# Input products of the state-space part for two chunks at once, and a closing sum moved

## The chip, the cores and the metric

The kernel runs on one core of one Trainium2 chip. The metric is the device time of one execution in microseconds (us), the median of several runs. Engines are named as in the profile: PE (TensorE, the matrix products), DVE (VectorE), ACT (ScalarE), POOL (GpSimd) and SP (SyncE, which issues most DMAs). L300 is line 300 of the kernel before.

## The reference

Two operators act on the same input x (2048 tokens by 1024 features), and a gate for each token mixes them.

```python
g = sigmoid((x * gate_w).sum(-1, keepdims=True))
a = irfft2(rfft2(x) * (w_r + 1j * w_i))            # a spectral filter over tokens and features
Lam_bar = exp(dt * Lam);  B_bar = ((Lam_bar - 1) / Lam)[:, None] * Bmat
Bu = einsum("bld,pd->blp", x, B_bar)               # 1024 complex states
h[t] = Lam_bar * h[t-1] + Bu[t]                    # 2048 steps
b = 2 * einsum("blp,dp->bld", h, Cmat).real + x * Dskip
return g * a + (1 - g) * b
```

The output is 2048 x 1024 in bfloat16.

## The kernel before, in words

**The spectral part** (`gfnet`) is a chain of short transforms. A front over 16 rows j turns x into the layout xQ (`turn_x`, PE transposes with a copy on ACT), folds it (DVE), and makes two transforms (`fd`, `s1`). `fd` leaves X1 by a copy out of PSUM (L339), on DVE for rows 3, 5 and 7 and on ACT for the others. `s1` leaves A (L351), on DVE for the first eight rows and on ACT for the last eight, and SP stores A to DRAM (L353). Four buffers hold A of the last eight rows, so A of row 12 waits until A of row 8 is stored. Then come 16 groups g of the inverse transform over tokens (`is1`), each with loads of the filter W, two products with it on DVE ("quotients", L468 and L469) and a store; then 16 half groups (`is2`), which leave ZT. From ZT, `spectral` makes the result for one tile of 128 tokens: eight products (L601), a scaled copy on ACT (L604) and four adds on DVE (L606 to L610).

**The state-space part** cuts the 2048 tokens into 8 chunks c of 256 and the 1024 states into two halves q, so that there are 16 quarters (c, q). `unit(c, q)` makes B x for one quarter in two steps (real and imaginary part): 4 blocks of 8 products of 256 columns (L300) into a PSUM buffer of 128 x 1024, and one copy on ACT into the tile h (L302). Two such PSUM buffers alternate (`psu`), and `early` and `spectral` take theirs from the same two. After the second step seven pieces of DVE work go onto the list `work`: `turn_back` (rotate by the angle of each state, L262, L263), `join`, two scans (L275), `carry_on` (the state carried into the next chunk), `turn` (rotate forth and scale, L286, L287), `join_on` (L292, L293). Then h is ready. Six tiles of h go round.

**Output.** For a tile tb of 128 tokens, which belongs to chunk tb // 2, `c_half` multiplies h by C: 16 products of 512 columns (L570) and 4 for the skip term (L574), for each half of the 1024 features. Tiles 0 to 9 are done by `early`: the result is scaled on ACT (L588) and stored to a scratch in DRAM. Their spectral sum is closed later by `late_tile`: `spectral` for that tile, and a DMA on POOL's queue that adds the scratch (L616); `close` stores it. These are the ten closing sums. Tiles 10 to 15 are done by `own_tile` at the end, with their spectral result added in PSUM, or on DVE for the last two.

**Order.** On PE, DVE and ACT the instructions run in the order in which the program writes them; the order on POOL and SP is a scheduler's. The generator `ssm` strings units and early tiles together, and the loops over the spectral part take one step of it (`halves(ssm, 1)`) at fixed places. `vector(us)` issues pieces from `work` until their noted costs make up that many microseconds; `vector_until(c)` issues what chunk c still needs. After `ssm` is used up, `spectral` for tile 10 is written ahead of the last units, and then:

```python
for _ in chain(unit(7, 0)):
    vector(4.0)
for n in (1, 1):
    halves(last, 1)          # last = unit(7, 1)
    vector(4.0)
    close_early(n)           # n closing sums
```

After that each half of an output tile is followed by `vector(4.0)` and by one closing sum or none.

`make_tab` makes tables of angles and decays for the quarters, and with them rz (L215, L216), the decay of each state along a chunk, on POOL.

Of the kernel before, what the change touches and what calls it, by code (L numbers as in the profile page):

```python
# [13 lines left out]
FP32 = mybir.dt.float32  # L14
BF16 = mybir.dt.bfloat16
# [8 lines left out]
P = 128  # L24
TC = 256
# [3 lines left out]
NHA, NHB = 4, 2  # L29
# [79 lines left out]
def kernel(  # L109
# [17 lines left out]
    nc = tc.nc  # L127
# [40 lines left out]
    pools = {"u": psF}  # L168
# [15 lines left out]
    BT = [btp.tile([P, 2, 8, P], BF16, name=f"BT{jb}") for jb in range(8)]  # L184
# [23 lines left out]
    def make_tab(jp):  # L208
        sh = [P, 2, TC]
        js = slice(2 * jp, 2 * jp + 2)  # L210
        ang = tmp.tile(sh, FP32, name="ang")
        for j in range(2):
            nc.vector.tensor_scalar_mul(out=ang[:, j], in0=tau_f, scalar1=thp[:, 2 * jp + j:2 * jp + j + 1])
            jb = 2 * jp + j
            nc.gpsimd.tensor_copy(out=rz[:, jb, :], in_=r_sb[:, jb:jb + 1].to_broadcast([P, TC]))  # L215
            nc.gpsimd.memset(rz[:, jb, 0:1], 0.0)  # L216
        sn_f = tmp.tile(sh, FP32, name="sn_f")
        cs_f = tmp.tile(sh, FP32, name="cs_f")
        yield from sincos(tmp, ang, sh, sn_f, cs_f, "rot")
        nc.gpsimd.tensor_copy(out=tab[:, 1, js, :], in_=sn_f)  # L220
        t1 = tmp.tile(sh, FP32, name="t1")
        t2 = tmp.tile(sh, FP32, name="t2")
        for j in range(2):
            nc.scalar.activation(out=t1[:, j], in_=sn_f[:, j], func=ACT.Copy, scale=ci[:, 2 * jp + j:2 * jp + j + 1])
        yield
        nc.gpsimd.tensor_copy(out=tab[:, 0, js, :], in_=cs_f)
        for j in range(2):
            jb = 2 * jp + j
            nc.scalar.activation(out=t2[:, j], in_=cs_f[:, j], func=ACT.Copy, scale=ci[:, jb:jb + 1])
            nc.vector.scalar_tensor_tensor(out=tab[:, 2, jb, :], in0=cs_f[:, j], scalar=cr[:, jb:jb + 1], in1=t1[:, j],  # L230
                                           op0=ALU.mult, op1=ALU.subtract)
        yield
        for j in range(2):
            jb = 2 * jp + j
            nc.vector.scalar_tensor_tensor(out=tab[:, 3, jb, :], in0=sn_f[:, j], scalar=cr[:, jb:jb + 1], in1=t2[:, j],
                                           op0=ALU.mult, op1=ALU.add)

    rz = tabp.tile([P, 8, TC], FP32, name="rz")
# [1 line left out]
    ck = cpool.tile([P, 2, 2, 8], FP32, name="ck")  # L240
    hs = {}
    hpool = [hpA, None]
    hcount = [0]

    def halloc(shape, dtype):
        pool = hpool[hcount[0] % (NHA + NHB) >= NHA]
        hcount[0] += 1
        return pool.tile(shape, dtype, name="h")

    work = []  # L250
    x_t = xQ.rearrange("p d j (g q) -> p d g j q", g=2)

    def unit(c, q):
        sh = [P, 2, 4, TC]
        u = halloc(sh, BF16)
        js = slice(4 * q, 4 * q + 4)
        bc = lambda i: tab[:, i:i + 1, js, :].to_broadcast(sh)
        tmps = {}

        def turn_back():  # L260
            su = up.tile(sh, BF16, name="su")
            nc.vector.tensor_mul(out=su, in0=u[:, ::-1], in1=bc(1))  # L262
            nc.vector.tensor_mul(out=u, in0=u, in1=bc(0))  # L263
            tmps["su"] = su

        def join():
            su = tmps["su"]
            nc.vector.tensor_add(out=u[:, 0], in0=u[:, 0], in1=su[:, 0])
            nc.vector.tensor_sub(out=u[:, 1], in0=su[:, 1], in1=u[:, 1])
            if c:  # L270
                nc.vector.tensor_add(out=u[:, :, :, 0], in0=u[:, :, :, 0], in1=carry[:, :, js])

        def scan(ri):
            seg = u[:, ri].rearrange("p j t -> p (j t)")
            nc.vector.tensor_tensor_scan(out=seg, data0=rz[:, js].rearrange("p j t -> p (j t)"), data1=seg,  # L275
                                         initial=0.0, op0=ALU.mult, op1=ALU.add)

        def carry_on():
            if c + 1 < NCH:
                gl = u[:, :, :, TC - 1]  # L280
                nc.vector.tensor_mul(out=ck[:, :, :, js], in0=gl.unsqueeze(1).to_broadcast([P, 2, 2, 4]), in1=rot[:, :, :, js])
                nc.vector.tensor_add(out=carry[:, :, js], in0=ck[:, :, 0, js], in1=ck[:, :, 1, js])

        def turn():
            sg = up.tile(sh, BF16, name="sg", tag="su")
            nc.vector.tensor_mul(out=sg, in0=u[:, ::-1], in1=bc(3))  # L286
            nc.vector.tensor_mul(out=u, in0=u, in1=bc(2))  # L287
            tmps["sg"] = sg

        def join_on():  # L290
            sg = tmps["sg"]
            nc.vector.tensor_add(out=u[:, 0], in0=u[:, 0], in1=sg[:, 0])  # L292
            nc.vector.tensor_sub(out=u[:, 1], in0=u[:, 1], in1=sg[:, 1])  # L293
            hs[c, q] = u

        for ri in range(2):
            psu = pools["u"].tile([P, 4, TC], FP32, name="psu", tag="psu")
            for j in range(4):
                for d8 in range(8):
                    nc.tensor.matmul(psu[:, j, :], lhsT=BT[4 * q + j][:, ri, d8, :],  # L300
                                     rhs=x_t[:, d8, :, :, 8 * c:8 * (c + 1)], start=(d8 == 0), stop=(d8 == 7))
            nc.scalar.copy(out=u[:, ri].rearrange("p b (q j) -> p b q j", j=32),  # L302
                           in_=psu.rearrange("p b (j q) -> p b q j", j=32))
            if ri == 1:
                work.extend([(2.4, turn_back), (1.5, join), (2.3, lambda: scan(0)), (2.3, lambda: scan(1)),
                             (0.4, carry_on), (2.4, turn), (1.4, join_on)])
            yield 3.5

    owed = [0.0]

    def vector(us):
        owed[0] += us
        while work and owed[0] > 0:
            cost, piece = work.pop(0)
            piece()
            owed[0] -= cost
        if not work:
            owed[0] = min(owed[0], 0.0)
# [8 lines left out]
    def gfnet():  # L327
# [4 lines left out]
        def fd(j):  # L332
            ps = psA.tile([P, 2, K], FP32, name="ps_fd", tag="ps")
            for cls in range(2):
                for d4 in range(4):
                    nc.tensor.matmul(ps[:, cls, :], lhsT=preTs[j][:, 4 * cls + d4, :], rhs=G_sb[:, cls, d4, :],  # L336
                                     start=(d4 == 0), stop=(d4 == 3))
            X1 = gta.tile([P, 2, K], BF16, name="X1")
            (nc.vector.tensor_copy if j in (3,5,7,) else nc.scalar.copy)(out=X1.rearrange("p r (i c) -> p r i c", c=2), in_=ps.rearrange("p c (r i) -> p r i c", r=2))  # L339
            X1s[j] = X1  # L340

        def s1(j):
# [236 lines left out]
    def early(tb):  # L579
        psy = pools["u"].tile([P, D], FP32, name="ps_y", tag="psu")  # L580
        for hf in range(2):
            c_half(psy, tb, hf)
            if hf == 0:
                load_xs(tb + 1)
                yield 3.7
        for hf in range(2):
            ye = fft["lp"].tile([P, K], FP32, name="ye", bufs=2)
            nc.scalar.activation(out=ye, in_=psy[:, K * hf:K * (hf + 1)], func=ACT.Copy, scale=omg[:, tb:tb + 1])  # L588
            nc.sync.dma_start(out=y_dram[tb, hf], in_=ye)
        yield 3.7  # L590
# [157 lines left out]
    def chain(*items):  # L748
        for item in items:
            yield from item  # L750
# [2 lines left out]
        for _ in range(n):  # L753
            next(gen, None)

    ssm = chain(unit(0, 0), unit(0, 1), unit(1, 0), unit(1, 1), unit(2, 0), early(0), unit(2, 1), early(1), unit(3, 0), early(2), unit(3, 1), early(3), unit(4, 0), early(4), unit(4, 1), early(5), unit(5, 0), early(6), unit(5, 1), early(7), unit(6, 0), unit(6, 1), early(8), early(9))

    order = {
        **{j: [(load_B, n)] for j, n in ((2, 1), (3, 1), (4, 1), (5, 2), (6, 2), (7, 2), (8, 2), (9, 2))},
# [45 lines left out]
    nc.vector.scalar_tensor_tensor(out=thp, in0=dt, scalar=INV2PI, in1=lim, op0=ALU.mult, op1=ALU.mult)  # L805
    r_sb = sp.tile([P, 8], FP32, name="r_sb")
    nc.scalar.activation(out=r_sb, in_=are, func=ACT.Exp)
    tau_f = tmp.tile([P, TC], FP32, name="tau_f")
    nc.vector.tensor_copy(out=tau_f, in_=tau_i)

# [103 lines left out]
            yield v  # L914

    ga[NEARLY] = spectral(NEARLY, grat, own_home(NEARLY))
    last = unit(7, 1)

    def close_early(n):
        for _ in range(n):  # L920
            close(2)
            late_tile(late.pop(0))

    for _ in chain(unit(7, 0)):
        vector(4.0)
    for n in (1, 1):
        halves(last, 1)
        vector(4.0)
        close_early(n)
    for tb in range(NEARLY + 1, 16):  # L930
        xs[tb] = xQ.rearrange("p d (k j) m -> p (d k) (j m)", k=2)[:, tb].rearrange("p (d m) -> p d m", m=P)
        nc.sync.dma_start_transpose(out=xs[tb], in_=x[P * tb:P * (tb + 1), :])
    for tb, counts in ((10, (1, 1)), (11, (1, 1)), (12, (1, 1)), (13, (1, 1)), (14, (0, 0)), (15, (0, 0))):
        for _, n in zip(own(tb), counts):
            vector(4.0)
            close_early(n)
            if not late:
                close(0)
# [31 lines left out]
```

## Time and profile before

| | |
|---|---|
| median of 5 runs | 341.35 us (340.33 to 342.35) |
| profiled execution | 342.25 us, of which the span of the profile is 340.5 us |
| granted clock of PE | 0.998 |
| busy: PE, DVE, ACT, POOL | 327.7, 291.5, 166.9, 32.6 us |
| PE products of 256 columns (L300) | 1024 |
| copies of 128 x 1024 out of PSUM behind them (L302) | 32, 1011 ns each |

Stages, in us of the span: the front to about 88.7, a stretch of small steps to 126.4, the 16 groups of `is1` to about 203, `is2` and the rest of `ssm` to 262, the last units to 279.5, the output tiles 10 to 15 to 336.9, the last store to 340.5.

How the lines are read: a group line gives engine, operation, output and inputs with their shapes, count, busy time, mean length of one, and the idle time of the engine just before. A timeline line gives start, length, engine, line and operation, count, and in brackets how long the engine had stood idle before it and what released it. Lengths of products overlap, since they are pipelined; the spacing of starts is what one costs. The chain of work that ended last gives start and length of each piece.

### The profile page before, as it was taken

The page shows a single profiled execution, that of the slowest core. Times are in us where ns is not written, and L with a number is a line of the kernel's source. Part 1 is how long each engine was busy: PE and PEld are TensorE (multiplying, and loading weights), DVE is VectorE, ACT ScalarE, POOL GpSimd, SP SyncE. Part 2 cuts the span into 40 slices and gives each one's busy share as a digit, 9 for nine tenths or more (in the row PEclk, how much of TensorE's full clock was granted, in tenths as well). Part 3 has the DMA queues.
Part 4 walks back from the last instruction along what each step waited for, and adds up shares of the span by engine and source line. Part 5 has one row for each costly group of instructions (what it writes and reads, how often), then busy time and mean ns, then how long its engine had stood idle before and what let it go on. Part 6 is the DMA issues. An engine that isn't in the chain of part 4 may idle for free.

```text
span 340.5 us, 6233 instructions
## 1 busy us (share of the span) xinstructions
PE 327.7 (96%) x2446; PEld 212.0 (62%) x2446; DVE 291.5 (86%) x449; ACT 166.9 (49%) x211; POOL 32.6 (10%) x64
## 2 busy tenths in 40 slices
PE   7989899969999999999999999999999999999995
PEld 3445465746858584756666485869955875565552
DVE  2679949969999999999999999999980997999951
ACT  3697597834432145765566452546632242433410
POOL 1372012120000000000000000000000011122220
PEclk9999999999999999999999999999999999999999
DMA  7999999999996036988999954948103109946695
GB/s 264 379 206 150 231 224 208 124 188 240 257 274 118 2 92 177 227 227 228 268 233 295 233 155 128 239 130 218 62 2 102 54 22 142 178 93 109 107 141 169
DMA packets 83581, 58.71 MB, mean 172 GB/s; under 512 B 54328, under 2 KB 74304, under 8 KB 83424
## 3 DMA queue, kind: packets, MB, share of 16 engines
q1 hardware_dynamic: 80304, 55.64, 66.8%
q0 software_dynamic: 3168, 2.66, 8.2%
q8 instruction: 19, 0.31, 0.4%
q14 instruction: 10, 0.08, 0.1%
q10 hardware_dynamic: 80, 0.01, 0.0%
HBM read 30.49 MB, written 17.83 MB: 142 GB/s over the span
## 4 chain that ended last, share of the span: by engine, by line
PE 70%; DVE 21%; DMA 3%; ACT 2%; issue 2%; SPq 1%; DVEq 0%; ACTq 0%
PE ps_y L570 26%; PE psu L300 22%; PE ps_h L570 4%; DVE h L275 4%; PE ps_id L601 4%; PE ps_is L509 2%; PE ps_is L485 2%; PE ps_s L460 2%; PE ps_is L484 2%; DVE CT L351 2%; PE ps_fd L336 2%; DMA G_sb<-c_G 2%; PE ps_y L574 2%; DMA turn_scratch<-A 1%; DVE h L263 1%
## 5 line engine op out<-in xcount | busy, mean ns | idle before, releaser
L300 PE MATMUL psu<-xQ,BT 128*128 128x256 bf16 x1024 | 116.6, 273 | 0.8 <-ACT ye L588 0.5
L300 PEld LDWEIGHTS <-BT 128*128 128x128 bf16 x1024 | 98.9, 98 | 17.5 <-issue 4.5
L570 PE MATMUL ps_y<-CT,h 128*128 128x512 bf16 x448 | 101.3, 379 | 0.0
L570 PEld LDWEIGHTS <-h 128*128 128x128 bf16 x512 | 49.6, 98 | 55.2
L275 DVE TENSOR_TENSOR_SCAN h<-rz,h 128x1024 bf16<-128x1024 f32 x32 | 72.2, 2280 | 0.3
L302 ACT CAST h<-psu 128x1024 bf16<-128x1024 f32 x32 | 32.3, 1011 | 51.4 <-PE psu L300 51.3
L616 POOL DMA_DIRECT2D BT<-y_scratch x10 | 11.9, 1194 | 239.6 <-DVE BT L610 232.0
L588 ACT ACTIVATE ye<-ps_y,omg 128x512 f32<-128x512 f32 x20 | 12.7, 684 | 43.1 <-PE ps_y L574 28.7
L336 PE MATMUL ps_fd<-G_sb,preT 128*128 128x512 bf16 x128 | 30.4, 379 | 1.9 <-ACT X L339 1.0
L262 DVE TENSOR_TENSOR su<-h,tab 128x2048 bf16<-128x2048 bf16 x16 | 19.6, 1223 | 2.8 <-ACT h L302 2.2
L336 PEld LDWEIGHTS <-preT 128*128 128x128 bf16 x128 | 12.0, 98 | 15.6 <-issue 3.1
L462 ACT CAST X<-ps_s 128x1024 bf16<-128x1024 f32 x16 | 16.2, 1014 | 8.6 <-PE ps_s L460 8.6
L263 DVE TENSOR_TENSOR h<-h,tab 128x2048 bf16<-128x2048 bf16 x16 | 19.6, 1225 | 0.8
L287 DVE TENSOR_TENSOR h<-h,tab 128x2048 bf16<-128x2048 bf16 x16 | 19.6, 1225 | 0.5
L286 DVE TENSOR_TENSOR sg<-h,tab 128x2048 bf16<-128x2048 bf16 x16 | 19.5, 1218 | 0.1
L657 ACT COPY xQ<-pt 128x1024 bf16<-128x1024 bf16 x16 | 15.6, 1016 | 2.3 <-PE pt L656 2.2
L511 ACT CAST ZT<-ps_is 128x1024 bf16<-128x1024 f32 x16 | 15.5, 1023 | 2.2 <-PE ps_is L509 2.2
L339 ACT CAST X<-ps_fd 128x1024 bf16<-128x1024 f32 x13 | 13.2, 1014 | 6.1 <-PE ps_fd L336 6.1
L487 ACT CAST C<-ps_is 128x1024 bf16<-128x1024 f32 x16 | 16.1, 1008 | 0.0
L601 PE MATMUL ps_id<-raw,ZT 128*128 128x256 bf16 x128 | 15.9, 273 | 0.0
L570 PE MATMUL ps_h<-CT,h 128*128 128x512 bf16 x64 | 14.5, 379 | 0.0
L601 PEld LDWEIGHTS <-ZT 128*128 128x128 bf16 x128 | 12.4, 98 | 2.2
(186 smaller groups left out, 363.6 us busy)
## 6 DMA issues: line engine op xcount, KB each, us to landing
y_scratch<-ye SPq DMA_DIRECT2D x20, 256.0 KB, 2.7
CT<-in_A_x_dram SPq DMA_DIRECT2D x8, 512.0 KB, 6.1
Bb<-turn_scratch SPq DMA_DIRECT2D x16, 256.0 KB, 4.0
turn_scratch<-C SPq DMA_DIRECT2D x16, 256.0 KB, 3.8
raw<-turn_scratch SPq DMA_DIRECT2D x16, 256.0 KB, 4.0
Wb<-in_A_w_r_dram SPq DMA_DIRECT2D x32, 127.8 KB, 4.0
Wb<-in_A_w_i_dram SPq DMA_DIRECT2D x32, 127.8 KB, 4.0
out_dram<-BT SPq DMA_DIRECT2D x14, 256.0 KB, 3.1
```

Of the source, the lines that this page charges most:

```text
L262: nc.vector.tensor_mul(out=su, in0=u[:, ::-1], in1=bc(1))
L263: nc.vector.tensor_mul(out=u, in0=u, in1=bc(0))
L275: nc.vector.tensor_tensor_scan(out=seg, data0=rz[:, js].rearrange("p j t -> p (j t)"), data1=seg, initial=0.0, op0=ALU.mult, op1=ALU.add)
L286: nc.vector.tensor_mul(out=sg, in0=u[:, ::-1], in1=bc(3))
L287: nc.vector.tensor_mul(out=u, in0=u, in1=bc(2))
L300: nc.tensor.matmul(psu[:, j, :], lhsT=BT[4 * q + j][:, ri, d8, :], rhs=x_t[:, d8, :, :, 8 * c:8 * (c + 1)], start=(d8 == 0), stop=(d8 == 7))
L302: nc.scalar.copy(out=u[:, ri].rearrange("p b (q j) -> p b q j", j=32), in_=psu.rearrange("p b (j q) -> p b q j", j=32))
L336: nc.tensor.matmul(ps[:, cls, :], lhsT=preTs[j][:, 4 * cls + d4, :], rhs=G_sb[:, cls, d4, :], start=(d4 == 0), stop=(d4 == 3))
L462: nc.scalar.copy(out=X2, in_=ps2)
L487: nc.scalar.copy(out=C1.rearrange("p h (c i) -> p h c i", c=2), in_=psc.rearrange("p h (i c) -> p h c i", c=2))
L570: nc.tensor.matmul(psy, lhsT=hs[c, jb // 4][:, ri, jb % 4, P * tq:P * (tq + 1)], rhs=CT[ri][:, jb, 512 * dh:512 * (dh + 1)], start=(i == 0 ...
L601: nc.tensor.matmul(pse[:, slot, :], lhsT=ZT_t[:, i, tb, :], rhs=fft["Gi"][:, i, :], start=(kb == 0), stop=(kb == 1))
```

## The change

From chunk 2 on, `pair(k, q)` takes the place of the units of chunks 2k and 2k + 1. It has four steps (real and imaginary part, each with two of the four blocks), each of 16 products of 512 columns, which are the tokens of both chunks in one, and two copies on ACT, one into h of each chunk. The DVE work of both chunks goes onto `work` after the fourth step, that of chunk 2k first. The order of the quarters on DVE becomes (2,0), (3,0), (2,1), (3,1), (4,0), (5,0), (4,1), (5,1), (6,0), (7,0), (6,1), (7,1). The number of steps in `ssm` is 48 as before. Early tiles now come two after another. Which of the six tiles of h a quarter takes is written in a table. The last pair is (3, 1), with a closing sum behind its second, third and fourth step; tile 13 has one less. X1 is copied by ACT in all rows. rz is written in one place ahead of the tables.

```diff
-            jb = 2 * jp + j
-            nc.gpsimd.tensor_copy(out=rz[:, jb, :], in_=r_sb[:, jb:jb + 1].to_broadcast([P, TC]))
-            nc.gpsimd.memset(rz[:, jb, 0:1], 0.0)
...
-    def halloc(shape, dtype):
-        pool = hpool[hcount[0] % (NHA + NHB) >= NHA]
-        hcount[0] += 1
-        return pool.tile(shape, dtype, name="h")
+    slots = {(0, 0): 0, (0, 1): 1, (1, 0): 2, (1, 1): 3, (2, 0): 4, (3, 0): 5, (2, 1): 0, (3, 1): 1,
+             (4, 0): 2, (5, 0): 3, (4, 1): 4, (5, 1): 0, (6, 0): 5, (7, 0): 1, (6, 1): 2, (7, 1): 4}
+
+    def halloc(c, q, shape, dtype):
+        slot = slots[c, q]
+        return hpool[slot >= NHA].tile(shape, dtype, name="h", tag=f"h{slot}", bufs=1)
...
+    def pair(k, q):
+        both = [pieces(2 * k + i, q) for i in range(2)]
+        for ri in range(2):
+            for h in range(2):
+                psu = pools["u"].tile([P, 2, 2 * TC], FP32, name="psu", tag="psu")
+                for j in range(2):
+                    for d8 in range(8):
+                        nc.tensor.matmul(psu[:, j, :], lhsT=BT[4 * q + 2 * h + j][:, ri, d8, :],
+                                         rhs=x_t[:, d8, :, :, 16 * k:16 * (k + 1)], start=(d8 == 0), stop=(d8 == 7))
+                for i in range(2):
+                    nc.scalar.copy(out=both[i][0][:, ri, 2 * h:2 * h + 2].rearrange("p b (q j) -> p b q j", j=32),
+                                   in_=psu.rearrange("p b (j q) -> p b q j", j=32)[:, :, 8 * i:8 * (i + 1)])
+                if ri == 1 and h == 1:
+                    for u, todo in both:
+                        work.extend(todo)
+                yield 3.5
...
-            (nc.vector.tensor_copy if j in (3,5,7,) else nc.scalar.copy)(out=X1.rearrange("p r (i c) -> p r i c", c=2), in_=ps.rearrange("p c (r i) -> p r i c", r=2))
+            nc.scalar.copy(out=X1.rearrange("p r (i c) -> p r i c", c=2), in_=ps.rearrange("p c (r i) -> p r i c", r=2))
...
-    ssm = chain(unit(0, 0), unit(0, 1), unit(1, 0), unit(1, 1), unit(2, 0), early(0), unit(2, 1), early(1), unit(3, 0), early(2), unit(3, 1), early(3), unit(4, 0), early(4), unit(4, 1), early(5), unit(5, 0), early(6), unit(5, 1), early(7), unit(6, 0), unit(6, 1), early(8), early(9))
+    ssm = chain(unit(0, 0), unit(0, 1), unit(1, 0), unit(1, 1), pair(1, 0), early(0), early(1), pair(1, 1), early(2), early(3), pair(2, 0), early(4), early(5), pair(2, 1), early(6), early(7), pair(3, 0), early(8), early(9))
...
+    for jb in range(8):
+        nc.gpsimd.tensor_copy(out=rz[:, jb, :], in_=r_sb[:, jb:jb + 1].to_broadcast([P, TC]))
+        nc.gpsimd.memset(rz[:, jb, 0:1], 0.0)
...
-    last = unit(7, 1)
+    last = pair(3, 1)
...
-    for _ in chain(unit(7, 0)):
-        vector(4.0)
-    for n in (1, 1):
+    for n in (0, 1, 1, 1):
         halves(last, 1)
         vector(4.0)
         close_early(n)
...
-    for tb, counts in ((10, (1, 1)), (11, (1, 1)), (12, (1, 1)), (13, (1, 1)), (14, (0, 0)), (15, (0, 0))):
+    for tb, counts in ((10, (1, 1)), (11, (1, 1)), (12, (1, 1)), (13, (1, 0)), (14, (0, 0)), (15, (0, 0))):
```

The seven pieces of DVE work, once inside `unit`, are now in `pieces(c, q)`, unchanged, which `unit` and `pair` both call.

More of the change, by code (lines that the diff above doesn't have):

```diff
@@ L242, with pieces @@
     hpool = [hpA, None]
-    hcount = [0]
-    def halloc(shape, dtype):
-        pool = hpool[hcount[0] % (NHA + NHB) >= NHA]
-        hcount[0] += 1
-        return pool.tile(shape, dtype, name="h")
+    slots = {(0, 0): 0, (0, 1): 1, (1, 0): 2, (1, 1): 3, (2, 0): 4, (3, 0): 5, (2, 1): 0, (3, 1): 1,
[3 more added lines that the diff above has]
+        return hpool[slot >= NHA].tile(shape, dtype, name="h", tag=f"h{slot}", bufs=1)
     work = []
     x_t = xQ.rearrange("p d j (g q) -> p d g j q", g=2)
-    def unit(c, q):
+    def pieces(c, q):
         sh = [P, 2, 4, TC]
-        u = halloc(sh, BF16)
+        u = halloc(c, q, sh, BF16)
         js = slice(4 * q, 4 * q + 4)
@@ L294, in join_on, with unit @@
             hs[c, q] = u
+        return u, [(2.4, turn_back), (1.5, join), (2.3, lambda: scan(0)), (2.3, lambda: scan(1)),
+                   (0.4, carry_on), (2.4, turn), (1.4, join_on)]
+    def unit(c, q):
+        u, todo = pieces(c, q)
         for ri in range(2):
@@ L304, in unit @@
             if ri == 1:
-                work.extend([(2.4, turn_back), (1.5, join), (2.3, lambda: scan(0)), (2.3, lambda: scan(1)),
-                             (0.4, carry_on), (2.4, turn), (1.4, join_on)])
+                work.extend(todo)
             yield 3.5
+    def pair(k, q):
[12 more added lines that the diff above has]
+                    for u, todo in both:
+                        work.extend(todo)
+                yield 3.5
     owed = [0.0]
```

## The prediction

> **What bounds the kernel now.** I read the page's busy shares and chain first, then the groups by line, then each engine's timeline around the edited places. The page:
>
> ```profile
> PE 327.7 (96%) x2446; PEld 212.0 (62%) x2446; DVE 291.5 (86%) x449; ACT 166.9 (49%) x211; POOL 32.6 (10%) x64
> PE 70%; DVE 21%; DMA 3%; ACT 2%; issue 2%; SPq 1%; DVEq 0%; ACTq 0%
> L300 PE MATMUL psu<-xQ,BT 128*128 128x256 bf16 x1024 | 116.6, 273 | 0.8 <-ACT ye L588 0.5
> L570 PE MATMUL ps_y<-CT,h 128*128 128x512 bf16 x448 | 101.3, 379 | 0.0
> L302 ACT CAST h<-psu 128x1024 bf16<-128x1024 f32 x32 | 32.3, 1011 | 51.4 <-PE psu L300 51.3
> L588 ACT ACTIVATE ye<-ps_y,omg 128x512 f32<-128x512 f32 x20 | 12.7, 684 | 43.1 <-PE ps_y L574 28.7
> ```
>
> PE is busy 96% of 340.5 us and carries the chain; nearly all its idle time lies in the first 81 us and in the 3.6 us after its last product. So the end moves by what PE gains or loses per product, and by any new place where it stands still. The chain in order of time prices products by spacing, not by their pipelined length:
>
> ```profile
> 111.57 3.45 PE ps_y L570 x16
> 119.32 3.49 PE psu L300 x32
> ```
>
> Sixteen products of 512 columns take 3.45 us, thirty-two of 256 take 3.49: 215.6 and 109.1 ns each. The weight loads (98 ns) lie under the products in both.
>
> Idle PE time of the first part has a cause outside the edit (timelines of SP, ACT, PE):
>
> ```profile
> 67.64 1.25 SPq L353 DMA_DIRECT2D turn_scratch<-A  x1
> 72.77 1.01 ACT L351 CAST A<-ps_s 128x1024 bf16<-128x1024 f32 x1 [5.53 <-DMA turn_scratch<-A]
> 73.83 0.61 PE L348 MATMUL ps_s<-X,raw 64*128 64x512 bf16 x4 [2.81 <-ACT A L351]
> ```
>
> A store stands in SP's queue until 67.64, lands at 72.7, ACT waits 5.53, PE 2.81, and DVE 2.68 for the same ACT copy. What ACT, DVE or PE lose or gain by up to about 2.7 us before that is taken up there.
>
> The third reading is the end of the state-space work (timelines of DVE, PE):
>
> ```profile
> 264.40 0.42 DVE L606 TENSOR_TENSOR raw<-raw 128x512 bf16<-128x512 bf16 x1 [9.81 <-ACT raw L604]
> 273.89 1.04 PE L601 MATMUL ps_id<-raw,ZT 128*128 128x256 bf16 x8
> 275.16 3.65 PE L300 MATMUL psu<-xQ,BT 128*128 128x256 bf16 x32 [0.23 <-ACT h L302]
> 285.63 0.42 DVE L606 TENSOR_TENSOR raw<-raw 128x512 bf16<-128x512 bf16 x1 [1.75 <-ACT raw L604]
> 300.33 3.62 PE L570 MATMUL ps_y<-CT,h 128*128 128x512 bf16 x16
> 300.63 0.68 DVE L293 TENSOR_TENSOR h<-h,sg 128x1024 bf16<-128x1024 bf16 x1
> ```
>
> From 264.4 DVE works through three quarters, in the old order (6,1), (7,0), (7,1), with the sums of the output tiles between. Its second and third lines show what a product right behind a closing sum costs: the sum takes 0.87, the next step starts 1.27 after it, so 0.40 is lost. The last two lines are the decisive pair: output tile 12 starts on PE at 300.33, and the second of DVE's three quarters ends at 301.31. Before, that second one was (7,0), which tile 12 doesn't read.
>
> **The change, part by part.**
>
> *Products.* 768 of 256 columns become 384 of 512, in 24 steps as before: 24 x (3.49 - 3.45) = 0.96 us less, 0.80 of it in the five pairs ahead of the last. Weight loads halve, but they were hidden. No row shows 512 columns gathered in pieces of 16 elements. L300 gathers in pieces of 8, and two of its products take 218.2 ns against 215.6 for one of L570, which reads without gaps: gathering costs next to nothing, so I take the L570 price; bounds -0.96 to 0.
>
> A rule to weigh: the Trainium skill's "TensorE: Matmul & The Clock Gate", section "Back-to-back issue gap", gives about 131 ns a product as the sustained price at 512 columns with weight loads. By it the 384 products would take 50 us instead of 84 and the change would gain over 30 us; the row says 215.6 ns under just such loads, so I set the rule aside.
>
> *Copies out of PSUM.* One copy of 1024 columns (1.01 us) becomes two of 512. The nearest row is one copy of 512 at 0.586 us (L701); successive ones overlap by 0.1 (the two of L588, 0.684 each, take 1.27 together). So 1.07 us, at most 1.27. ACT is at 49% and each step has 3.5 us, so 24 x 0.06 costs nothing by itself; it counts only where PE waits for the buffer. The same skill's "ScalarE: Activation LUTs", section "What ACT_TABLE_LOAD costs", charges 186 ns + 0.833 N with 93 ns overlap, which makes 1.13 us of the two; that rule speaks against splitting, and the difference from 1.07 is too small to matter.
>
> *The closing sum moved forward.* Before, one step stood right behind a closing sum (0.40 lost); now two do, each with 0.06 more: 2 x 0.46 - 0.40 = 0.5 us, at most 0.9 with the longer copies. The sum's own 0.87 of PE only moves, from tile 13 to the last pair. Its scaling on ACT (1.11), its four DVE adds (278.61 - 277.15 = 1.46) and its accumulating DMA on POOL's queue move along. POOL has idled since 75 us, and its wait of 7.3 us for a store stays one closing sum earlier; the next store on SP waits for the same accumulations as before. These are off the path, save for the adds below.
>
> *The new order of quarters.* Until 254 us DVE works without a break, so the n-th quarter ends about when the n-th did. Early tile 4 now needs the third one behind chunk 1; that ended at 169.4, and tile 4 takes the place of the step that began at 176.26 (L300): 6 us spare. Early tile 8 has over 15. The quarters of pair (3, 0) begin about 4 us later, eaten out of the idle 9.81. Tile 12 is where it turns: it now needs (6,1), second of DVE's last three. PE gets to tile 10 at 279.52 - 0.96 + 0.5 + 0.87 = 279.93, 0.41 later. DVE's adds for tile 11 hang on PE, so they start at 285.63 + 0.41 = 286.04 (DVE gets there at 284.5, so the wait of 1.75 shrinks to 1.5). From there to the end of the second quarter it was 301.31 - 285.63 = 15.68 us, with three sums between, as now: (6,1) ends at 301.72. PE would begin tile 12 at 300.74, so it waits 1.0 us. All of the rest of the program is queued behind on PE. Bounds: 0 if DVE is a microsecond ahead, 2.5 if one more sum of 1.46 gets in between. Tile 14 needs (7,1), done at 319.4 before, 1.7 us ahead of it; both move alike.
>
> *X1 of rows 3, 5, 7 on ACT.* DVE loses three copies of 1.22; ACT gains three of 1.01 (0.91 apart). ACT idles 2.0 us between 23 and 30 us (0.40, 0.87, 0.77), so of the 2.7 between 0.7 and 2.7 arrives at X1 of row 8 and at PE's next product, which waited 1.03 for it already; I take 1.7. DVE's lead is lost at 45.3, where it waits 3.27 for ACT. The stop at 72.7 covers all of it: zero. Uncovered, +1.7.
>
> *rz.* All eight copies ran back to back on POOL from 10.81 to 14.2 already, ahead of a wait of 4.4 us: zero.
>
> *Sum.* -0.96 + 0.5 + 1.0 = +0.54; the 0.87 of the moved sum is added ahead of tile 12 and taken away behind it. The profiled execution took 342.25 us, so 342.8; it lies 0.9 above the median, and on the median of 341.35 that makes 341.9.
>
> **The rivals.**
>
> *Slower: SP's queue at the paired early tiles.* Early tiles now come two after another. Each brings 1.33 us of transpose issue and 1.0 of stores on SP. A group of the inverse transform costs SP about 3.6 us in 4.9 (four W loads near 0.63, one load and one store near 0.54). Four groups with one early tile: 16.7 of 19.6 us; with two: 19.1. In the trace the DMA share there is 0.82 and the W loads are never late; the quotients' products have 0.9 to 3 us of slack on DVE. It decides once SP falls 2 us behind, since the weights are buffered three deep; then both such stretches cost about 1.5 each: +3.0, 344.9.
>
> *Slower: the front is not covered.* If the store at 67.64 moves with ACT's delay, 1.7 is added: 343.6. Against it: the store was ready at 44 and stood in the queue.
>
> *Faster: DVE's 3.4 us count.* Chain shares give DVE 21%, most of it before 107. If SP's queue is ordered anew with earlier copies, the 2.81 and 0.75 us of PE's waits shrink: about -3.0, 338.9. Against: DVE's two waits of 3.27 and 2.68 us.
>
> *Nothing happens:* the wide products run at 2 x 109 ns; then +1.5, 342.85.
>
> **How the numbers follow.** Forecast 0.46, nothing 0.08, queue 0.19, front 0.12, faster 0.15. Half a per cent (1.7 us) is about what a measurement can tell from no change: below 339.65 or above 343.05. Faster: 0.15. Slower: 0.19 + 0.08 of the front + 0.04 of the first two: 0.31. Same: 0.54. The range of the likeliest is 340.6 to 343.2; out to the rivals, 339.8 to 344.9, which leaves out most of the faster case and half of the queue's, 0.2 in all.
>
> **What would show it.** Right: L300's successor with steps of 3.45; two waits of about 0.3 to 0.5 us for h at the last pair; a wait of about 1 us for DVE h at tile 12's first product; PE's stop near 73 us shorter than 2.81. Wrong: PE waiting for the quotients or DVE for W between 130 and 195; the store of A issued later than 68; no wait at tile 12.

## The result and the profile after

The changed kernel takes 341.31 us (median; 340.36 to 343.91), the kernel before 340.54 us in the same job (339.55 to 343.98): a ratio of 1.0021, with a 95% interval of 1.001 to 1.0033. The change costs 0.8 us, clear of zero by this interval; two later measurements of the same kernel, with fewer runs, gave 1.0014 and 1.0022, with intervals that take in 1. The forecast was 341.9 us and "same". The number held; three of its terms did not, and they nearly cancelled. Executions of one kernel lie up to 4.4 us apart, and the profiled one may be any of them: that of the changed kernel took 343.61 us (span 341.8), that of the kernel before 342.25, which is 2.3 and 1.7 us above their medians. So kernels are compared below stage by stage, and not by spans alone.

The page of the changed kernel, its busy shares, the chain by engine, and the two groups that take the place of L300 and L302 (L317 is the product of `pair`, L320 its copy):

```profile
PE 329.0 (96%) x2062; PEld 175.4 (51%) x2062; DVE 289.1 (85%) x446; ACT 171.1 (50%) x238; POOL 32.5 (10%) x64
PE 80%; ACT 7%; DVE 6%; SPq 3%; issue 2%; DMA 1%; ACTq 0%; DVEq 0%
L317 PE MATMUL psu<-xQ,BT 128*128 128x512 bf16 x384 | 85.9, 379 | 1.1 <-ACT h L320 0.6
L320 ACT CAST h<-psu 128x512 bf16<-128x512 f32 x48 | 25.8, 589 | 46.4 <-PE psu L317 46.4
```

The change did what it says: 384 products fewer (2446 - 2062), DVE 2.4 us less busy, ACT 4.2 us more, and 37 us less of weight loads that had been hidden. PE is as busy as before. Its idle time in front of L317 is 1.1 us in all, 0.6 of it for ACT's copies, and those are two places at the end. DVE's share of the chain is 6% here and was 21%, but that is no effect of the change. When both kernels were profiled again (e8 the kernel before, e9 the changed kernel), their chains read, in this order:

```profile
PE 72%; DVE 22%; ACT 2%; issue 2%; DMA 1%; DVEq 0%; ACTq 0%
PE 68%; DVE 20%; ACT 6%; issue 3%; DMA 2%; SPq 0%; DVEq 0%; ACTq 0%
```

The share follows the execution; the change moves it little.

The chain in order of time prices a step of `pair` as before an output tile's:

```profile
120.99 3.45 PE psu L317 x16
```

The last pair and the place where the forecast saw a wait (timelines of PE and DVE: start, length, engine, line, operation, count, and in brackets the idle time ahead with its releaser):

```profile
271.37 1.04 PE L619 MATMUL ps_id<-raw,ZT 128*128 128x256 bf16 x8
272.70 3.61 PE L317 MATMUL psu<-xQ,BT 128*128 128x512 bf16 x16 [0.29 <-ACT h L320]
276.15 1.04 PE L619 MATMUL ps_id<-raw,ZT 128*128 128x256 bf16 x8
277.47 3.61 PE L317 MATMUL psu<-xQ,BT 128*128 128x512 bf16 x16 [0.29 <-ACT h L320]
302.61 3.62 PE L588 MATMUL ps_y<-CT,h 128*128 128x512 bf16 x16
303.20 0.69 DVE L290 TENSOR_TENSOR h<-h,sg 128x1024 bf16<-128x1024 bf16 x1
```

Two closing sums are followed 1.33 and 1.32 us later by the next step, so each loses 1.33 - 0.87 = 0.46 us: the forecast's figure. Tile 12 starts at 302.61 with nothing in brackets, although quarter (6, 1) is only done at 303.89. The forecast wait of 1.0 us is not there.

Four kernels by stage, from PE's timeline. The marks are the start of the small products `zps` (L420 before, L438 after; the end of the front and of what follows it), the start of the spectral sum for tile 10 (where the last units begin) and the end of PE's last product; the rest of the span is the tail. E8 is the kernel before and e9 the changed kernel, both run again unaltered; e10 and e11 are experiments told below.

| us | start of zps | zps to tile 10's sum | to the end of PE | tail | span |
|---|---|---|---|---|---|
| e8, before | 105.57 | 154.42 | 75.03 | 3.6 | 338.6 |
| e9, changed | 106.42 | 153.96 | 75.39 | 3.5 | 339.3 |
| e10, changed, X1 of three rows on DVE | 105.37 | 153.97 | 75.38 | 3.7 | 338.4 |
| e11, changed, closing sums late | 106.03 | 153.97 | 74.49 | 4.2 | 338.7 |

The changed kernel gains 0.46 us in the long middle, loses 0.36 in the last stretch, and loses 0.85 ahead of zps: +0.7 us of span for 0.8 of the medians. The second and third columns repeat to 0.04 us in every execution profiled of kernels with the same code there (one exception, told at e1). The first does not, and e8 and e9 are one execution each, on two chips. The theory to be tested was that its loss is X1's three copies on ACT.

### The profile page after: what moved, and what is told of

Same layout as the page of the kernel before. It is cut to its first block, busy times and chain, and to the rows that moved or that the text cites. A ratio compares the mean times of both kernels' runs of the same rounds, so it can differ in the third digit from the quotient of the medians.

```text
span 341.8 us, 5499 instructions
## 1 busy us (share of the span) xinstructions
PE 329.0 (96%) x2062; PEld 175.4 (51%) x2062; DVE 289.1 (85%) x446; ACT 171.1 (50%) x238; POOL 32.5 (10%) x64
## 4 chain that ended last, share of the span: by engine, by line
PE 80%; ACT 7%; DVE 6%; SPq 3%; issue 2%; DMA 1%; ACTq 0%; DVEq 0%
PE ps_y L588 28%; PE psu L317 24%; PE ps_h L588 4%; PE ps_id L619 3%; PE ps_fd L354 3%; SPq L573 3%; PE psu L302 2%; PE ps_is L527 2%; PE ps_s L478 2%; PE ps_is L503 2%; PE ps_is L502 2%; PE ps_y L592 2%; ACT xQ L675 2%; ACT X L357 1%; PE pt L674 1%
## 5 line engine op out<-in xcount | busy, mean ns | idle before, releaser
L317 PE MATMUL psu<-xQ,BT 128*128 128x512 bf16 x384 | 85.9, 379 | 1.1 <-ACT h L320 0.6
L317 PEld LDWEIGHTS <-BT 128*128 128x128 bf16 x384 | 37.2, 98 | 44.6 <-issue 1.6
L320 ACT CAST h<-psu 128x512 bf16<-128x512 f32 x48 | 25.8, 589 | 46.4 <-PE psu L317 46.4
L302 PE MATMUL psu<-xQ,BT 128*128 128x256 bf16 x256 | 30.4, 279 | 0.0
L302 PEld LDWEIGHTS <-BT 128*128 128x128 bf16 x256 | 25.0, 100 | 7.1 <-issue 3.4
L357 ACT CAST X<-ps_fd 128x1024 bf16<-128x1024 f32 x16 | 16.2, 1015 | 5.9 <-PE ps_fd L354 5.9
```

The costliest lines, as they stand in the source:

```text
L317: nc.tensor.matmul(psu[:, j, :], lhsT=BT[4 * q + 2 * h + j][:, ri, d8, :], rhs=x_t[:, d8, :, :, 16 * k:16 * (k + 1)], start=(d8 == 0), sto ...
L320: nc.scalar.copy(out=both[i][0][:, ri, 2 * h:2 * h + 2].rearrange("p b (q j) -> p b q j", j=32), in_=psu.rearrange("p b (j q) -> p b q j", ...
L357: nc.scalar.copy(out=X1.rearrange("p r (i c) -> p r i c", c=2), in_=ps.rearrange("p c (r i) -> p r i c", r=2))
```

## The experiments

**Products of 256 columns in the pairs (e4).** Only the products were put back; steps, buffers, order and the number of copies are those of the changed kernel. The copies (not shown) read the buffer in the order in which these products leave it, at 588 ns each against 589.

```diff
-                    for d8 in range(8):
-                        nc.tensor.matmul(psu[:, j, :], ...
-                                         rhs=x_t[:, d8, :, :, 16 * k:16 * (k + 1)], ...)
+                    for i in range(2):
+                        for d8 in range(8):
+                            nc.tensor.matmul(psu[:, j, TC * i:TC * (i + 1)], ...
+                                             rhs=x_t[:, d8, :, :, 16 * k + 8 * i:16 * k + 8 * (i + 1)], ...)
```

> The changed kernel with products of 256 columns in the pairs, in the same four steps, same PSUM buffers and copies. By the price of the products (0.04 us for each of 24 steps, 0.80 us of it ahead of the last pair) it is 0.96 us slower than the changed kernel: ratio to before 1.005. If the width of the products is worth nothing on PE (weight loads were hidden), no different from the changed kernel.

Measured: 341.85 us, 1.0024 (1.0001 to 1.0048) of the kernel before, 0.54 above the unaltered changed kernel (e1) on the same chip. The profile is sharper: zps to tile 10's sum takes 154.60 us against 153.96, and the end 75.55 against 75.39. That is 0.64 = 16 x 0.04 for the 16 steps in the middle and 0.16 = 4 x 0.04 for the last four. A step is back at 3.49 us in e4's chain: the wide product is worth just the 0.04 us a step that the chain showed. The four steps of pair (1, 0) lie ahead of zps, where PE waits for DVE anyway, and count for nothing.

**The changed kernel unaltered (e1, e9) and the kernel before unaltered (e8).**

> The changed kernel once more, unaltered, for an undisturbed profile beside a time: its profiled execution of 343.61 us had a granted clock of 0.50 between 82 and 84 us. Both theories: 0.7 us above before (ratio 1.002). Theory F (front): the three X1 copies on ACT cost about 1.2 us before 91 us and the rest of the program gains about 0.5. Theory L (late): the front is covered by the stores and the loss arises after 91 us. In an undisturbed profile the first wide product starts at 89.1 (as before) by L, and at 90 to 90.5 by F.

> The kernel before, unaltered, for a second profile: the first one was of an execution of 342.25 us, 1.7 above the median of 80 runs. If the store of A lands at 72.7 only in such an execution, ACT's copy of A for row 12 begins at 70 to 71 here and PE and DVE wait less than 1 us for it; if it is the rule, at 72.7 again. Ratio 1.000.

> The changed kernel unaltered, to stand on one chip beside the two edits that were measured apart before (X1 of rows 3, 5, 7 on DVE, 0.95 us faster; closing sums placed late, only 0.45 us faster though its last stretch is 0.90 shorter) and beside both together. Theory A: the two edits act in different places and add up, 0.9 each; the sums' small result came of the front, which costs more or less by the execution. Theory B: sums placed late give away in the middle what they gain at the end, about 0.5. Here: 1.002 of the kernel before (341.2 us where that takes 340.5).

Measured: e1 341.31 us, 1.0014 (0.9991 to 1.0038); e8 340.41, 0.9991 (0.9976 to 1.0005); e9 341.54, 1.0022 (0.9994 to 1.0051). E8 settled what the prediction had taken as given. In the profile of before, ACT's copy of A(12) waited 5.53 us for a store and PE 2.81 for that copy. In e8 the same two lines (timelines of ACT and DVE; the second is the first scan of quarter (0, 1)) read:

```profile
69.09 1.01 ACT L351 CAST A<-ps_s 128x1024 bf16<-128x1024 f32 x1 [1.68 <-DMA turn_scratch<-A]
76.62 4.47 DVE L275 TENSOR_TENSOR_SCAN h<-rz,h 128x1024 bf16<-128x1024 f32 x2
```

The copy stands at 69.09 instead of 72.77 and waited 1.68 us, and DVE's scan starts at 76.62 instead of 78.48. Of the other profiles here, one alone (e5) has the copy as late as 72.80. So the late store belonged to the execution that happened to be profiled, and the cover with it. E5 (told below) keeps X1 on ACT and has the late stop, and there the cover works as the prediction had it (timelines of ACT and PE):

```profile
72.80 1.01 ACT L369 CAST A<-ps_s 128x1024 bf16<-128x1024 f32 x1 [4.52 <-DMA turn_scratch<-A]
107.49 0.56 PE L438 MATMUL zps<-Bcol,K_sb 32*128 32x16 bf16 x16
```

It reaches zps at 107.49, the profiled execution of before at 107.43 (one execution each). When SP issues that store does not follow X1's copies: it is at 62.76 to 67.64 in the six profiles with three of them on DVE, and at 63.02 to 67.70 in the eight with all of them on ACT.

E1's profile has a stretch of 155.65 us where the others have 153.96 to 154.00; that is the clock, told at the end.

**X1 of rows 3, 5 and 7 back on DVE (e2, e10), and on ACT in the kernel before (e3).**

```diff
-            nc.scalar.copy(out=X1...
+            (nc.vector.tensor_copy if j in (3,5,7,) else nc.scalar.copy)(out=X1...
```

E3 is the same edit the other way round in the kernel before.

> The changed kernel with X1 of rows 3, 5 and 7 back on DVE. Theory F: faster than the changed kernel by about 1.2 us, so 0.5 us faster than before (ratio 0.9985). Theory L: no different from the changed kernel (ratio 1.002).

> X1 of rows 3, 5, 7 on DVE. Both theories: 0.9 us under the unaltered changed kernel, first scan of quarter (0, 1) on DVE at about 76.5 instead of 77.6.

> The kernel before with X1 of all rows on ACT and nothing else changed. Theory F: 1.2 us slower than before (ratio 1.0035). Theory L: no difference (ratio 1.000), since ACT's wait for the stores of A takes the delay up.

Measured: e2 340.36 us, 0.95 under e1 on its chip; e10 340.14, 1.40 under e9 on its chip; e3 341.31, equal to e1 and 0.5 above its kernel before (1.0013, 0.9994 to 1.0033). E9 and e10 ran on one chip; PE's and DVE's timelines of e9:

```profile
39.28 1.89 PE L354 MATMUL ps_fd<-G_sb,preT 128*128 128x512 bf16 x8 [1.59 <-ACT X L357]
77.47 4.46 DVE L272 TENSOR_TENSOR_SCAN h<-rz,h 128x1024 bf16<-128x1024 f32 x2
106.42 0.54 PE L438 MATMUL zps<-Bcol,K_sb 32*128 32x16 bf16 x16 [0.37 <-DVE Bcol L431]
```

and of e10:

```profile
38.08 1.89 PE L354 MATMUL ps_fd<-G_sb,preT 128*128 128x512 bf16 x8 [1.03 <-ACT X L357]
76.43 4.47 DVE L272 TENSOR_TENSOR_SCAN h<-rz,h 128x1024 bf16<-128x1024 f32 x2
105.37 0.54 PE L438 MATMUL zps<-Bcol,K_sb 32*128 32x16 bf16 x16 [1.85 <-DVE Bcol L431]
```

The three extra copies make the fold's product on PE 1.20 us later, and 1.04 of it is still there at DVE's scan and 1.05 at zps, which waits for DVE's Bcol in both. In e3 the scan starts at 77.66, against 76.62 in e8. Between e10 and e9 nothing from 38 to 106 us takes the delay up: DVE works through a list there whose end PE waits for. The size varies with the execution, the sign does not. In the profiles without the late stop the scan starts at 76.26 to 76.64 with three copies on DVE (five profiles) and at 76.94 to 78.20 with all on ACT (seven). Zps starts at 105.22 to 105.59 and at 105.89 to 107.22, leaving out the first profile of the changed kernel (108.90), which has a stretch of lower clock ahead of it, told at the end.

**Closing sums late (e5, e11), and with X1 back on DVE (e7, e12).** No closing sum stands in the last pair but behind its fourth step; tile 13 has two and tile 14 one.

```diff
-    for n in (0, 1, 1, 1):
+    for n in (0, 0, 0, 1):
...
-    ... (13, (1, 0)), (14, (0, 0)), (15, (0, 0))):
+    ... (13, (1, 1)), (14, (1, 0)), (15, (0, 0))):
```

> The changed kernel with no closing sum behind the second and third step of the last pair: one behind the fourth, and one each behind the halves of tiles 10 to 13 and the first half of tile 14. By the price of a step right behind a closing sum (0.45 us each in the changed kernel's profile) it is 0.9 us faster than the changed kernel, 340.4. If the end of the state-space work on DVE sets the time of tiles 12 to 15, the two waits only move there: no difference.

> Closing sums late alone. Theory A: 0.9 us under the unaltered changed kernel (340.3). Theory B: 0.4 under it, with the stretch from zps to the end of PE longer elsewhere.

> The changed kernel with X1 of rows 3, 5 and 7 on DVE and the closing sums of e5: the two gains added, 0.95 + 0.9 us below the changed kernel, 339.5, which would be 1 us faster than the kernel before. If the two are not independent, about 340.2.

> Both edits. Theory A: 1.8 us under the unaltered changed kernel, 0.997 of the kernel before. Theory B: 1.3 under it, 0.9985.

Measured: e5 340.86 us and e11 340.77 (0.77 under e9); e7 339.91 and e12 341.05. PE's timeline of e5 shows the four steps of the last pair as one unbroken row of 64 products; the first sum stands behind them, at 276.85:

```profile
263.04 13.97 PE L317 MATMUL psu<-xQ,BT 128*128 128x512 bf16 x64 [0.53 <-ACT ye L606]
```

On PE the end is 74.49 us in all four instead of 75.39: the 0.90 that two losses of 0.46 explain. Yet from zps to the end of the span, tail included, e11 is only 0.2 us shorter than e9, and e5 not at all. (The medians put e11 0.77 under e9; but the profiled e11 also came to zps 0.39 earlier, with the same code there, so the front's spread is in that figure.) In neither theory was the reason, and it lies behind PE's last product: the tail is 4.2 to 4.4 us in these four kernels and 3.5 to 3.7 in all others. E9's last accumulation and last store (timelines of POOL and SP), with the last of DVE's work:

```profile
324.46 1.19 POOL L634 DMA_DIRECT2D BT<-y_scratch  x1 [1.80 <-DVE BT L628]
335.81 0.75 DVE L661 SCALAR_TENSOR_TENSOR BT<-ps_h,omg,raw 128x512 bf16<-128x512 f32 x1 [2.92 <-PE ps_h L592]
336.58 0.33 SPq L663 DMA_DIRECT2D out_dram<-BT  x1
```

and e11's:

```profile
327.63 1.19 POOL L634 DMA_DIRECT2D BT<-y_scratch  x1 [3.54 <-DVE BT L628]
334.52 0.75 DVE L661 SCALAR_TENSOR_TENSOR BT<-ps_h,omg,raw 128x512 bf16<-128x512 f32 x1 [2.92 <-PE ps_h L592]
334.92 0.33 SPq L642 DMA_DIRECT2D out_dram<-BT  x1
335.82 0.40 SPq L663 DMA_DIRECT2D out_dram<-BT  x1
```

With a sum in tile 14 the last accumulation is issued at 327.63. SP's store of that tile (L642) starts only at 334.92, 7.3 us behind that issue, and the stores of the last tile stand behind it in the queue. DVE is done at 335.27 and its store starts 0.55 us later; in e9 it started 0.02 later. With 0.2 us more from the start of the last store to the end of the span, that is the 0.7 us. So in these profiles the placement of the changed kernel, which loses 0.46 twice on PE, gets most of it back at the other end.

E7 had looked like a version that beats both kernels (0.9973, 0.9954 to 0.9993). E12 is the same kernel on another chip and gave 1.0000 (0.9972 to 1.0028), although its profiled execution took 339.98 us and its stages are e7's within 0.4 us. By the medians the X1 edit was worth 0.95 us from e5 to e7 and -0.28 from e11 to e12. Part of that is PE's clock, whose mean is on record for every timed execution: five of e12's twelve have 0.995 or less (341.40 to 342.02 us), and none of e11's. With the executions of 0.997 or more alone, e12's median is 340.37, and the X1 edit is worth 0.39 there, 0.86 from e5 to e7, 0.77 from e1 to e2, 1.05 from e9 to e10, and e3 is 0.64 above its kernel before: five pairs, one sign. By the same count e12 is level with its kernel before (340.34), so that any version here beats the kernel before is not shown.

**The other half of the states first (e6).** In e6 every output tile reads its second half of the states first.

```diff
-            jb, ri = i // 2, i % 2
+            jb, ri = (i // 2 + 4) % 8, i % 2
```

> The changed kernel with the products of every output half in another order: states of half 1 first. By the recorded step tile 12 waits for the quarter (6, 1) at its first product already, so nothing changes. By the reading of the changed kernel's profile (tile 12 starts at 302.61, the quarter ends at 303.89, and only its ninth product reads it) a wait of 1.3 us appears at tile 12 and the kernel is 1.3 us slower than the changed one, 342.6.

Measured: 341.98 us, 1.0059 (1.0035 to 1.0084), against 1.0014 and 1.0022 for the changed kernel. PE's timeline at tile 12:

```profile
298.69 1.04 PE L619 MATMUL ps_id<-raw,ZT 128*128 128x256 bf16 x8
300.30 0.39 PE L588 MATMUL ps_y<-CT,h 128*128 128x512 bf16 x1 [0.57 <-DVE h L289]
300.90 2.33 PE L588 MATMUL ps_y<-CT,h 128*128 128x512 bf16 x10 [0.21 <-DVE h L290]
```

Here is the wait that was forecast: 0.57 us for the first piece of `join_on` of (6, 1) and 0.21 for the second. By the spacing of starts they cost 300.30 - 298.69 - 0.87 = 0.74 and 0.60 - 0.22 = 0.38 us, and that is the whole difference: the last stretch takes 76.52 us, 1.13 more than the 75.39 of the changed kernel. With the half done first the wait is not there at all, since eight products of 0.2156 us lie between the start of the tile and the first read of (6, 1): in the changed kernel that read comes at 302.61 + 1.72 = 304.33, behind 303.89. The lead is 0.44 us.

## Why the prediction was right, and where it was not

The forecast time and the class were right; that they were is largely luck, as the terms show.

*Products: the price was right, the place was not.* Forecast -0.96. The 0.04 us a step is exact (e4), and gathering in pieces of 16 elements costs nothing that shows: 3.45 us, as L570. But only what lies behind zps counts. The middle should give 16 x 0.04 = 0.64 and gave 0.46: the stretch behind zps holds one early half of 3.68 us (3.45 + 0.23) more and one step of 3.49 less than before, another 0.19. With 0.16 in the last pair, 0.62 arrived. The failed step is "0.80 of it in the five pairs ahead of the last", counted without asking whether PE was waiting for DVE behind the first of them.

*Closing sums: right.* Forecast +0.5 against -0.16 of the wide products, +0.34; the last stretch is 0.36 longer.

*Tile 12: the term of 1.0 us was 0.* The quarter was as late as forecast against the tile (1.28 us behind its start; the forecast had 0.98). The failed step is "it now needs (6,1)", taken as needed at the tile's start: `c_half` reads the four blocks of half 0 in its first eight products. The forecast named the bounds 0 to 2.5, with 0 only if DVE were early. The right reason for 0 was in the loop's order. E6 takes it away and shows the wait. The prediction had named "no wait at tile 12" as a sign of being wrong, and by that sign it was.

*The front: the term of 0 was about 1.* The failed step is "the stop at 72.7 covers all of it": right for the profiled execution, as e5 shows, but only e5 of 13 other profiles has that stop. The delay at PE's fold was forecast as 1.7 us if uncovered, and measured 1.20 (39.28 against 38.08). At zps 1.05 of it is left from e10 to e9, 0.99 from e2 to e1, and 0.44 from e12 to e11. So the rival "the front is not covered" is what happened, at about half its price and by another condition: the rival wanted the store at 67.64 to move with ACT, and the store's time does not follow ACT's copies; in most executions there is no such long stop to hide behind.

*The sum.* With the front's 0.85 of the one pair e8 and e9, -0.62 + 0.5 + 0 + 0.85 = +0.73, against the forecast +0.54 and the measured +0.77. The front alone varies by more than these differ, so the close agreement is no proof of the terms; e4, e6 and the X1 pairs are. Three terms were off, by -1.0 (tile 12), +0.85 (front) and +0.34 (products), and together by only +0.19. That is luck: the forecast number is no evidence for its steps, since two of the four were wrong by more than the whole effect.

*The other rivals.* SP's queue at the paired early tiles cost nothing: the stretch that holds all of them is 0.46 shorter, which leaves no room for two stalls of 1.5 us. "DVE's 3.4 us count" was the wrong way round: in e9 and e10 DVE's list sets zps, but giving it less work made zps later, since ACT, which feeds it, came later. "Nothing happens" is excluded by the step of 3.45 us and by e4.

## What to carry to other kernels

Before a delay is called covered by a wait, see whether the wait is in a second execution: of 13 other profiles one had the late store that was to cover this one, and there alone it did. A tile needs a buffer when its first product reads it, not when the tile starts: half a tile of other work is a lead of 1.7 us, and it can be read in the loop. Where work is moved away from the end of PE's list, follow the queue behind PE too, since the last accumulation and the stores behind it have an end of their own.

## What the runs showed of the hardware

PE's granted clock was lower behind short pauses, in some executions only. In the changed kernel's profile ACT waited 6.05 us for the store of A and PE 2.53 us for ACT (timelines of ACT and PE):

```profile
79.86 1.01 ACT L369 CAST A<-ps_s 128x1024 bf16<-128x1024 f32 x1 [6.05 <-DMA turn_scratch<-A]
80.92 1.03 PE L366 MATMUL ps_s<-X,raw 64*128 64x512 bf16 x4 [2.53 <-ACT A L369]
81.89 4.78 PE L302 MATMUL psu<-xQ,BT 128*128 128x256 bf16 x32
```

and the windows (span of the window, its length, busy time and count of PE, weight loads, DVE, ACT and POOL, then the granted clock, the DMA share and GB/s):

```profile
80.00:82.00 2.00, 1.08 (x5) 0.24 (x5) 2.00 (x1) 2.00 (x3) 0.00 (x0) 0.70 0.96 286
82.00:84.00 2.00, 2.00 (x11) 1.39 (x10) 1.90 (x5) 1.62 (x2) 0.00 (x0) 0.50 0.83 193
```

Around the end of the pause and behind it the granted clock is 0.70 and then 0.50. The four products of L366 take 1.03 us where they take 0.61 at full clock (e9), and the step of L302 4.78 where it takes 3.67: 1.5 us lost, beside the pause. In e1 a pause of 1.59 us ahead of zps (106.52) was followed by a clock of 0.62 from 108 to 112, and the stretch behind it was 1.7 us longer than in all other profiles of that code.

The Trainium skill's "TensorE: Matmul & The Clock Gate", section "HAM oscillation — how this bites in real kernels", has as its rule that PE should have no idle gaps over about 3.4 us. Here gaps of 2.53 and 1.59 us were followed by a lower clock, while pauses of 2.81 us (before) and 1.89 us (e4) were not. The measurement decides: a pause of 1.6 us was followed by the loss of its own length once more, and whether that happens differs by the execution. That the pause is the cause is not shown; these are the only two stretches of lower clock in the 14 profiles ahead of PE's last product. The mean clocks on record show what such executions make of the spread. Of the 68 timed executions of the changed kernel, 12 have a mean clock of 0.995 or less, with a median of 343.03 us, and 56 have 0.997 or more, with 341.25. For the kernel before it is 10 of 114, with 343.10 against 340.46. That is a part of the spread and not all of it: one execution of before with a mean clock of 1.0 took 343.35.
